# Attention and two feed-forward layers on one core: probability transposes ahead of the scores in odd steps, and another order of the PSUM pools

## The chip, the core and the metric

The kernel runs on one core of a Trainium2 chip. The metric is the device time of one launch in microseconds (us). Three runs of the kernel before gave 614.35, 614.77 and 615.74, median 614.77. TensorE (PE) multiplies and transposes and can write only to PSUM, here eight banks of 128 x 512 fp32; VectorE (DVE) and ScalarE (ACT) read PSUM; GpSimd (POOL) works in SBUF; SyncE (SP) issues DMAs.

## The reference

```python
scores = scale * np.matmul(q, k.transpose(0, 1, 3, 2))   # 2 batches, 8 heads, 768 positions, 64 wide
keep = is_sink | in_window                               # 4 sink keys, window of 128
scores = np.where(keep, scores, -1000000000.0)
a = np.exp(scores - max); a = a / (sum + 1e-09)
x = (a @ v), heads side by side                          # 1536 x 512
h = np.maximum(x @ w_in, 0.0); x = h * h @ w_out         # 512 -> 2048 -> 512
h = x @ w_in2; out = (h * np.tanh(softplus(h))) @ w_out2
```

All inputs and the result are fp32. The feed-forward products run with each factor split into a high and a low fp32r part, three products for one.

## The kernel before, in words

**Attention.** The 1536 rows are 12 tiles of 128 (two batches of six). Each tile has four head pairs, so there are 48 pairs; with a window of 128 and a few sink keys a pair needs scores of 128 queries against 128 keys (first tile of a batch), 256 (second tile) or 208 (all others, in two halves of 64 queries). The loop at L574 is a software pipeline over steps n = -3 to 52, written out by hand; every engine's queue holds its instructions in the order in which the steps issue them. Step n issues, in this order:

- `emit_s` (L398): scores of pair n+4 on PE, two PSUM banks;
- `emit_exp` (L419): exp of pair n+3 on ACT, PSUM to SBUF;
- `emit_max` (L409): mask and row maximum of pair n+4 on DVE, in PSUM, with the value `nm` that the exp needs;
- in even steps `emit_rs` (L430, L431, DVE) and `emit_norm` (L439, POOL): the reciprocal sums and the normalisation of pairs n+2 and n+3;
- `emit_x` (L503 ACT, L504 and L506 POOL) when the tile of pair n-4 is complete: the tile's result `av` is copied to `xf` and split;
- in odd steps `emit_t` (L451): PE transposes the probabilities of pairs n-1 and n, 64 x 64 at a time, into two banks; the first transpose writes the first bank, the second the other, and so on in turn;
- in even steps `prep_rows` (L346; PE transposes q and k of a later tile into two banks, which ACT and DVE copy out, L354) where n = 2 modulo 4 and such a tile is left (n = 2, 6, ..., 38), and then `emit_av` (L488): the products of pairs n-4 and n-3 with v, summed in one bank per tile;
- `evac_t` (L466): the two banks of transposed probabilities are copied to SBUF, the first by ACT, the second by DVE. They are copied in step n itself for n = 1 modulo 4, and in step n+1 for n = 3 modulo 4.

**Feed-forward layers.** `moe` follows with its own order: for each block of 128 hidden units 12 products h (L195, one bank), the activation on ACT and DVE (L204 to L209), and 12 products o (L659, four banks that accumulate over a stage). The h of the first two blocks is computed inside the attention loop, in steps 46 and 48, in banks of the scores' pool (`early[0]`, `early[1]`); ACT squares it in the step after and DVE takes the low part (L209) in the second step after. So `moe` begins with the o products of block 0, then h of block 2, then o of block 1. The weights are loaded by SP, and converted by ACT and DVE (L128 to L171) all the while.

**PSUM.** Pools take banks in the order in which they are opened. Before: `ps_s` (scores and early h) banks 0 to 3, `ps_p` (all transposes) 4 to 6, `ps_a` (av) 7. When the attention's pools are closed, `ps_h` takes 0 to 3 and `ps_o` 4 to 7. Inside a pool, as the program is built, the tiles get the first bank, then the last, then the last but one and so on down to the second, and then the first again: scores 0, 3, 2, 1; transposes 4, 6, 5; the four o tiles 4, 7, 6, 5. A new tile in a bank waits until the last reader of the old one is done, across pools too. 96 score tiles come before the two early h, which therefore get the first and the last bank of `ps_s`. In the ring of three for the transposes each `emit_t` of a step 4t+1 has as its second bank the first bank of step 4t-1; `prep_rows` of step 4t+2 has as its second bank the first of step 4t+1; `emit_t` of step 4t+3 has as its second bank the first of `prep_rows`. All three of these first banks are copied out by ACT.

Of the kernel before, what the change touches and what calls it, by code (L numbers as in the profile page):

```python
# [16 lines left out]
PSUM = bass.MemoryType.PSUM  # L17
# [11 lines left out]
def kernel(  # L29
# [41 lines left out]
    def load_limits():  # L71
        for j, src in enumerate((n_sink, window)):
            nc.scalar.dma_start(out=raw_i[:, j, :], in_=src.bitcast(I32).partition_broadcast(1))
# [137 lines left out]

    att = ExitStack()
    apool = att.enter_context(tc.tile_pool(name="apool", bufs=1))
    ps_s = att.enter_context(tc.tile_pool(name="ps_s", bufs=4, space=PSUM, reuse_waits="tile"))
    ps_p = att.enter_context(tc.tile_pool(name="ps_p", bufs=3, space=PSUM, reuse_waits="tile"))
    ps_a = att.enter_context(tc.tile_pool(name="ps_a", bufs=1, space=PSUM, reuse_waits="tile"))

    tiles = [(b, i) for b in range(B) for i in range(NB)]
    qn, kn, vn = {}, {}, {}
# [1 line left out]
    def load_tile(t, names="qkv", halves=1):  # L221
        if t >= len(tiles):
            return
        b, i = tiles[t]
        hs = H // halves
        for nm in names:
            dst = {"q": qn, "k": kn, "v": vn}[nm]
            dst[b, i] = apool.tile([P, H, D], F32, tag=nm + "n", name=nm + "n", bufs=5 if nm == "v" else 3)
        for h in range(0, H, hs):
            for nm in names:  # L230
                src, dst = {"q": (q, qn), "k": (k, kn), "v": (v, vn)}[nm]
                nc.sync.dma_start(
                    out=dst[b, i][:, h : h + hs, :],
                    in_=src[b, h : h + hs, i * P : (i + 1) * P, :].rearrange("h p d -> p h d"),
                )
# [18 lines left out]
    def positions():  # L254
        make_identity(nc, ident)
        for dst, base, pattern, mult in (
            (rel, 0, [[-1, P]], 1), (col, 0, [[1, P]], 0), (relp, P, [[-1, P]], 1)
        ):
            nc.gpsimd.iota(
                dst, pattern=pattern, base=base, channel_multiplier=mult, allow_small_or_imprecise_dtypes=True  # L260
            )
            if dst is rel:
                nc.gpsimd.affine_select(
                    out=rel, in_=rel, pattern=pattern, base=base, channel_multiplier=mult,
                    compare_op=ALU.is_ge, fill=1.0e9,
                )
# [25 lines left out]
    def load_rest(t):  # L292
        if t >= len(tiles) or tiles[t][1] < 2:
            return
        b, i = tiles[t]
        x = vx[b, i] = apool.tile([KV, 2, H, D], F32, tag="vx", name="vx", bufs=4)
        for dst, r, r0, n in (
            (0, 0, 0, SK), (SK, 0, i * P, HQ), (0, 1, i * P - HQ, HQ), (HQ, 1, 0, SK)
        ):
            nc.sync.dma_start(  # L300
                out=x[dst : dst + n, r], in_=v[b, :, r0 : r0 + n, :].rearrange("h p d -> p h d")
            )
# [65 lines left out]
    def chunks(i):  # L368
        if i == 0:
            return ((None, 0), (None, 0))  # L370
        if i == 1:
            return ((0, P), (0, P))
        return ((0, P), (0, KV))
# [67 lines left out]
    def emit_t(group):  # L441
        banks = [ps_p.tile([P, 2, 2, 2, P // 2], F32, tag="pt", name="pt") for _ in range(2)]
        for s, (b, i, j) in enumerate(group):
            for e in range(2):
                for c in range(2):
                    for r in range(2):
                        o = chunks(i)[r][c]
                        if o is None:
                            continue
                        rows = slice(r * D, (r + 1) * D)  # L450
                        nc.tensor.transpose(  # L451
                            banks[r][:, s, c, e, :], pr[b, i][rows, 2 * j + e, o : o + P], ident[rows, rows]
                        )
        pts = apool.tile([P, 2, 2, 2, P], F32, tag="pts", name="pts", bufs=2)
        for s, p in enumerate(group):
            st["pts", p] = pts[:, s]
        st["evac"] = [(group, banks[r], pts[..., r * D : (r + 1) * D], r) for r in range(2)]
# [72 lines left out]
    with tc.manual_schedule():  # L530
        load_limits()
        nc.scalar.preload_act_table_set("natural_log_exp_and_others")
        load_tile(0, "qk", halves=2)
        load_tile(1, "qk")
        load_tile(2, "kq")
        load_tile(0, "v")
        load_tile(3, "kq")
        positions()
        load_tile(1, "v")
        load_tile(2, "v")  # L540
        load_rest(2)
        warm = apool.tile([P, P], F32, name="warm")
        nc.vector.memset(warm, 0.0)
        nc.vector.memset(one, 1.0)
        nc.gpsimd.memset(two, 2.0)
        for x in prs:
            nc.gpsimd.memset(x[:, :, WIN:], 0.0)
        for x in sums:
            nc.vector.memset(x, 1e-9)
        idle = ps_a.tile([P, P + 2], F32, tag="av", name="idle")  # L550

        def keep_warm(times):
            for _ in range(times):
                nc.tensor.matmul(idle[:, 0:P], lhsT=warm, rhs=warm, start=True, stop=True)  # L554

        keep_warm(WARM[0])
        limits(idle[:, P : P + 2])
        first_mask()
        prep(0, "q", 0)
        keep_warm(WARM[1])  # L560
        prep(0, "k", 0)
        keep_warm(WARM[2])
        emit_s(*pairs[0])
        emit_max(*pairs[0], 0)
        emit_max(*pairs[0], 1)
        prep(0, "q", 1)
        prep(0, "k", 1)
        emit_s(*pairs[1])
        emit_max(*pairs[1], 0)
        emit_max(*pairs[1], 1)  # L570
        second_mask()
        window_masks()
        emit_exp(*pairs[0])
        for n in range(-3, NPR + 5):  # L574
            at = {d: pairs[n + d] for d in range(-4, 5) if 0 <= n + d < NPR}
            last = {d for d in at if at[d][2] == NPAIR - 1}
            t, j = divmod(n, NPAIR)
            if 4 in at and n > -3:
                emit_s(*at[4])
            if 3 in at and n > -3:  # L580
                emit_exp(*at[3])
            if 4 in at and n > -3:
                emit_max(*at[4], 0)
            if 4 in at and n > -3:
                emit_max(*at[4], 1)
            if n % 2 == 0:
                split_x()
                group = [at[d] for d in (2, 3) if d in at]
                if group:
                    emit_rs(group)  # L590
                for p in group:
                    emit_norm(*p)
            if -4 in last:
                emit_x(*at[-4][:2])

            if n % 2:
                if 0 in at:
                    emit_t([at[-1], at[0]])
            else:
                if n >= 0 and j == 2:  # L600
                    prep_rows(t + 2)
                for d in (-4, -3):
                    if d in at:
                        emit_av(*at[d])
            for _ in range((2, 2, 0, 0)[j]):
                evac_t()
            if n in (-3, -2):
                prep(1, "qk"[n + 3])
            if n >= 0 and j == NPAIR - 1:
                load_tile(t + 4, "q", halves=1 + (t + 5 == len(tiles)))  # L610
                load_tile(t + 4, "k", halves=1 + (t + 6 >= len(tiles)))
                load_tile(t + 3, "v")
                load_rest(t + 3)
            if n in SINKS:
                sink_keys(SINKS[n])
            if n < 0:
                keep_warm(WARM[3])
            if n == 1:
                fast_flag()
            for fb in range(W1N):  # L620
                if n == IN_AT[fb]:
                    early[fb] = ps_s.tile([P, TS], F32, tag="s", name="h")
                    in_products(early[fb], wt[0, fb], 0)
                if n == IN_AT[fb] + 1:
                    ready[fb] = new_g(gpool)
                    relu_squared(early[fb], ready[fb][0])
                if n == IN_AT[fb] + 2:
                    low_part(early[fb], *ready[fb])
            for m, steps in PLAN.items():
                for step in steps.get(n, "").split():  # L630
                    getattr(blocks[m], step)()
# [416 lines left out]
```

## Time and profile before

| | |
|---|---|
| median of three runs | 614.77 us |
| the profiled execution: time, span of its instructions | 614.9 us, 613.1 us |
| PE busy | 605.3 us (99%) |
| DVE, ACT, POOL busy | 452.1, 349.8, 70.6 us |
| DMA | 49.47 MB, mean 81 GB/s |
| granted TensorE clock, mean | 0.999 |

The attention stage takes about the first 90 us of the span, the feed-forward layers the rest. The time is the span and what lies around it, 1.8 us here. In rows of a timeline the columns are start, duration, engine, line, operation, output<-inputs, shape and count, and in brackets how long the engine had been idle and what released it. A group of PE instructions can contain waits: eight score products of one form that mostly take 0.58 us and once 0.99 us have waited inside. The chain of waits lists what the end of the program goes back to, in order of time: start, duration, engine, tile, line, count. There a PE row counts from one end to the next, so its length is the pace, and added idle time shows as a longer row.

### The profile page before, as it was taken

What the parts mean: (1) busy time and instruction counts of PE and PEld (TensorE: products, weight loads), DVE (VectorE), ACT (ScalarE), POOL (GpSimd) and SP (SyncE); (2) the same over time, 40 slices, a digit from 0 to 9 for tenths busy, and PEclk for the clock granted to TensorE, in tenths of its full rate; (3) what the DMA queues carried; (4) which work ended last, traced back from release to release, by engine and by line L of the source; (5) the groups of instructions that cost most, each with busy time, mean ns of one, the idle gap of its engine ahead of it and who ended that gap; (6) DMA issues with size and microseconds to landing.
All of it is one profiled execution on the core that took longest, in us unless ns stands there. A gap on an engine that the chain in (4) does not pass through costs nothing.

```text
span 613.1 us, 10262 instructions
## 1 busy us (share of the span) xinstructions
PE 605.3 (99%) x3854; PEld 491.6 (80%) x3854; DVE 452.1 (74%) x951; ACT 349.8 (57%) x723; POOL 70.6 (12%) x103
## 2 busy tenths in 40 slices
PE   9999999999999999999999999999999999999996
PEld 6676778888888888888888888888888888888885
DVE  5888889999621111188899699999888778888784
ACT  5989876877643333277777555555454444544442
POOL 5889950000000000000000000000000000000000
PEclk9999999999999999999999999999999999999999
DMA  9989736666400000036666300000010000100001
GB/s 188 188 181 185 196 108 202 207 204 187 158 1 0 2 0 1 0 111 198 204 196 188 101 0 2 0 1 1 1 69 1 0 1 0 53 17 2 0 1 72
DMA packets 71707, 49.47 MB, mean 81 GB/s; under 512 B 49508, under 2 KB 66148, under 8 KB 71652
## 3 DMA queue, kind: packets, MB, share of 16 engines
q1 hardware_dynamic: 71360, 48.38, 28.8%
q8 instruction: 31, 0.51, 0.4%
q10 hardware_dynamic: 292, 0.39, 0.2%
q14 instruction: 24, 0.20, 0.1%
HBM read 45.61 MB, written 3.15 MB: 80 GB/s over the span
## 4 chain that ended last, share of the span: by engine, by line
PE 96%; ACT 2%; DMA 1%; DVE 1%; issue 0%; DVEq 0%; ACTq 0%; SPq 0%
PE o L659 43%; PE h L195 42%; PE s L398 4%; PE av L488 3%; PE pt L451 2%; PE tr L346 1%; PE idle L554 1%; DMA raw<-in_moe_w_out_dram 1%; ACT pr L419 0%; PE tr L328 0%; ACT pts L466 0%; DVE cv_r L142 0%; ACT h L205 0%; ACT xf L503 0%; ACT h L204 0%
## 5 line engine op out<-in xcount | busy, mean ns | idle before, releaser
L195 PE MATMUL h<-xh,wil 128*128 128x512 f32 x384 | 102.9, 390 | 0.0
L195 PE MATMUL h<-xl,wih 128*128 128x512 f32 x384 | 102.7, 389 | 0.0
L195 PE MATMUL h<-xh,wih 128*128 128x512 f32 x384 | 102.6, 389 | 0.0
L209 DVE TENSOR_TENSOR gl<-h,gh 128x512 fp32r<-128x512 f32 x48 | 33.2, 691 | 89.0 <-ACT gh L206 88.9
L195 PEld LDWEIGHTS h<-xl,wih 128*128 128x128 f32 x384 | 72.1, 188 | 15.0
L195 PEld LDWEIGHTS h<-xh,wih 128*128 128x128 f32 x384 | 72.1, 188 | 15.0
L195 PEld LDWEIGHTS h<-xh,wil 128*128 128x128 f32 x384 | 71.9, 188 | 15.0
L659 PE MATMUL o<-gh,wol 128*128 128x512 f32 x192 | 74.9, 390 | 0.6 <-ACT xf L503 0.5
L727 ACT ACTIVATE e<-t,small 128x512 f32<-128x512 f32 x48 | 34.8, 725 | 70.4 <-DVE t L723 70.4
L659 PE MATMUL o<-gl,woh 128*128 128x512 f32 x192 | 74.7, 389 | 0.0
L659 PE MATMUL o<-gh,woh 128*128 128x512 f32 x192 | 74.7, 389 | 0.0
L204 ACT ACTIVATE h<-h 128x512 f32<-128x512 f32 x48 | 28.0, 582 | 76.1 <-PE h L195 76.1
L659 PE MATMUL o<-wol,gh 128*128 128x512 f32 x176 | 68.5, 389 | 0.0
L659 PE MATMUL o<-woh,gl 128*128 128x512 f32 x176 | 68.5, 389 | 0.0
L659 PE MATMUL o<-woh,gh 128*128 128x512 f32 x176 | 68.5, 389 | 0.0
L743 ACT CAST gh<-t 128x512 fp32r<-128x512 f32 x44 | 27.4, 623 | 46.3 <-PE o L659 42.9
L148 DVE SCALAR_TENSOR_TENSOR cv_a<-cv_a,cv_r 128x512 int32<-128x512 int32 x64 | 44.7, 698 | 6.2
L209 DVE TENSOR_TENSOR gl<-t,gh 128x512 fp32r<-128x512 f32 x44 | 30.4, 690 | 19.8 <-ACT gh L743 19.8
L128 ACT ACTIVATE cv_a<-raw 128x512 f32<-128x512 f32 x63 | 42.4, 673 | 1.5 <-DMA raw<-in_moe_w_out_dram 0.9
L659 PEld LDWEIGHTS o<-gh,wol 128*128 128x128 f32 x192 | 36.0, 187 | 8.5 <-ACT xf L503 1.0
L419 ACT ACTIVATE pr<-s,nm 128x208 f32<-128x208 f32 (+2 forms) x96 | 40.8, 438 | 2.4 <-DVE nm L409 2.2
L439 POOL TENSOR_TENSOR pr<-pr,rs 128x416 f32<-128x416 f32 (+2 forms) x48 | 41.0, 875 | 10.0 <-DVE rs L431 5.3
(107 smaller groups left out, 1000.5 us busy)
## 6 DMA issues: line engine op xcount, KB each, us to landing
raw<-in_moe_w_in_dram SPq DMA_DIRECT2D x32, 512.0 KB, 4.0
raw<-in_moe_w_out_dram SPq DMA_DIRECT2D x32, 512.0 KB, 4.3
vn<-in_v_dram SPq DMA_DIRECT2D x12, 256.0 KB, 5.7
qn<-in_q_dram SPq DMA_DIRECT2D x10, 256.0 KB, 4.8
kn<-in_k_dram SPq DMA_DIRECT2D x9, 256.0 KB, 5.1
vx<-in_v_dram SPq DMA_DIRECT2D x16, 128.0 KB, 4.1
out_dram<-ob SPq DMA_DIRECT2D x8, 256.0 KB, 2.4
kn<-in_k_dram SPq DMA_DIRECT2D x6, 128.0 KB, 3.3
```

The costliest lines, as they stand in the source:

```text
L128: nc.scalar.activation(out=self.a, in_=high_words, func=AF.Copy, scale=2.0**-112)
L148: nc.vector.scalar_tensor_tensor(out=ai, in0=ai, scalar=3, in1=self.r, op0=ALU.logical_shift_left, op1=ALU.bitwise_or)
L195: nc.tensor.matmul(ph, lhsT=w[a][:, d, :], rhs=x[:, d, :], start=(m == 0 and d == 0), stop=(m == 2 and d == NDC - 1),)
L204: nc.scalar.activation(out=ph, in_=ph, func=AF.Relu)
L209: nc.vector.tensor_tensor(out=gl, in0=x, in1=f32(gh), op=ALU.subtract)
L398: nc.tensor.matmul(banks[e][qs, 0:w], lhsT=kt[r, j, q1], rhs=kt[r, j, k0 : k0 + w], start=True, stop=True, skip_group_check=True,)
L419: nc.scalar.activation(out=pr[b, i][:, 2 * j + e, 0:w], in_=banks[e][:, 0:w], func=AF.Exp, bias=nm[:, e : e + 1], scale=-1.0, accum_out=sm ...
L439: nc.gpsimd.tensor_tensor(out=x, in0=x, in1=rs.to_broadcast([P, 2, w]), op=ALU.mult)
L488: nc.tensor.matmul(av[b, i][e * D : (e + 1) * D, j, qs], lhsT=x[0:kv, 2 * j + e, :], rhs=pts[0:kv, c, e, qs], start=(j == 0 and m == 0), s ...
L659: nc.tensor.matmul(acc[sp][t], lhsT=a, rhs=x, start=(fb == 0 and m == 0), stop=(fb == NFB - 1 and m == 2),)
L727: nc.scalar.activation(out=e, in_=t, func=AF.Ln, bias=two)
L743: nc.scalar.copy(g_tiles(n)[0], et[n][1])
```

## The change

Two edits. The pool `ps_a` is opened ahead of `ps_s`: av is then in bank 0, the scores and early h in 1 to 4 (taken in the order 1, 4, 3, 2), the transposes in 5 to 7. `ps_h` and `ps_o` are opened as before and keep 0 to 3 and 4 to 7. And in odd steps `emit_t` is issued at the head of the step, ahead of `emit_s`; everything else keeps its place in the step, `evac_t` too.

```diff
     apool = att.enter_context(tc.tile_pool(name="apool", bufs=1))
+    ps_a = att.enter_context(tc.tile_pool(name="ps_a", bufs=1, space=PSUM, reuse_waits="tile"))
     ps_s = att.enter_context(tc.tile_pool(name="ps_s", bufs=4, space=PSUM, reuse_waits="tile"))
     ps_p = att.enter_context(tc.tile_pool(name="ps_p", bufs=3, space=PSUM, reuse_waits="tile"))
-    ps_a = att.enter_context(tc.tile_pool(name="ps_a", bufs=1, space=PSUM, reuse_waits="tile"))
...
             t, j = divmod(n, NPAIR)
+            if n % 2 and 0 in at:
+                emit_t([at[-1], at[0]])
             if 4 in at and n > -3:
                 emit_s(*at[4])
...
-            if n % 2:
-                if 0 in at:
-                    emit_t([at[-1], at[0]])
-            else:
+            if n % 2 == 0:
                 if n >= 0 and j == 2:
                     prep_rows(t + 2)
```

## Rows read from the trace of the kernel before

**Rows 1.** The page: busy time by engine, and the chain by engine.

```profile
PE 605.3 (99%) x3854; PEld 491.6 (80%) x3854; DVE 452.1 (74%) x951; ACT 349.8 (57%) x723; POOL 70.6 (12%) x103
...
PE 96%; ACT 2%; DMA 1%; DVE 1%; issue 0%; DVEq 0%; ACTq 0%; SPq 0%
```

**Rows 2.** Stages: length, busy us of PE, PEld, DVE, ACT, POOL, granted clock, DMA.

```profile
28.91:47.92 19.01, 18.84 (x438) 14.22 (x436) 16.02 (x72) 16.73 (x65) 16.29 (x21) 1.00 0.94 191
80.55:93.43 12.88, 12.15 (x121) 9.31 (x118) 11.65 (x21) 9.90 (x18) 4.01 (x5) 1.00 0.50 164
```

**Rows 3.** Chain of waits in the attention stage: start, us, what.

```profile
26.29 1.02 PE av L488 x16
...
33.74 0.51 PE s L398 x8
34.25 0.64 PE pt L451 x16
...
35.41 1.08 PE av L488 x32
...
38.16 0.20 PE tr L346
...
38.37 0.71 PE tr L346 x15
...
44.52 0.71 PE tr L346 x15
...
50.59 0.64 PE tr L346 x16
...
53.80 0.59 PE av L488 x8
54.39 0.92 PE s L398 x8
...
56.59 0.81 PE tr L346 x16
```

**Rows 4.** Timeline of DVE, the maximum of a step 4t+3.

```profile
34.30 0.38 DVE L409 CUSTOM_DVE_ANT_0 s<-s,mask_w 128x208 f32<-128x208 f32 x1 [0.51 <-PE s L398]
```

**Rows 5.** Timeline of ACT, steps 3, 16 and 17.

```profile
14.83 0.58 ACT L354 COPY kt<-tr 128x512 f32<-128x512 f32 x1 [0.20 <-PE tr L346]
...
34.77 0.43 ACT L419 ACTIVATE pr<-s,nm 128x208 f32<-128x208 f32 x1 [0.23 <-DVE nm L409]
...
35.61 0.58 ACT L466 COPY pts<-pt 128x512 f32<-128x512 f32 x1
...
37.73 0.58 ACT L466 COPY pts<-pt 128x512 f32<-128x512 f32 x1 [0.69 <-PE pt L451]
```

**Rows 6.** Timeline of PE, steps 22, 31 and 45.

```profile
44.11 0.87 PE L346 MATMUL tr<-ident,kn 64*128 64x64 f32 x8
...
58.42 0.73 PE L451 MATMUL pt<-ident,pr 64*128 64x64 f32 x16
...
78.60 0.94 PE L451 MATMUL pt<-ident,pr 64*128 64x64 f32 x16
```

**Rows 7.** Timeline of POOL, normalisation of pairs 30 to 33.

```profile
56.60 3.72 POOL L439 TENSOR_TENSOR pr<-pr,rs 128x512 f32<-128x512 f32 x4
```

**Rows 8.** Timeline where the feed-forward layers begin, PE and PE's weight loads.

```profile
89.77 0.50 PE L659 MATMUL o<-gh,wol 128*128 128x512 f32 x1
...
91.25 0.19 PEld L659 LDWEIGHTS o<-gh,wol 128*128 128x128 f32 x1 [0.95 <-ACT xf L503]
91.25 0.50 PE L659 MATMUL o<-gh,wol 128*128 128x512 f32 x1 [0.52 <-ACT xf L503]
...
93.43 1.09 PE L195 MATMUL h<-xh,wil 128*128 128x512 f32 x4
```

**Rows 9.** The same stretch on ACT and DVE.

```profile
90.61 0.59 ACT L503 COPY xf<-av 128x512 f32<-128x512 f32 x1
90.75 0.69 DVE L209 TENSOR_TENSOR gl<-h,gh 128x512 fp32r<-128x512 f32 x1
```

## The prediction

> **What bounds the kernel now.** I read the page first. PE is busy for 605.3 of 613.1 us and holds 96% of the chain that ended last [rows 1]: an edit moves the time only if it opens or closes a gap on PE. The second view was busy time by stages. The granted clock is 1.00, the 2.4 GHz level, both inside attention and where the feed-forward layers begin [rows 2], so I charge nothing for the clock. In attention ACT, POOL and DVE have 84 to 88% of the stage as busy time and PE 99%: PE sets the pace, but the others have little room. The third view, the chain of waits, gives PE's pace piece by piece [rows 3]. Free of waits, the scores of a 208-wide pair cost 0.51, the transposes of two pairs 0.64, av 1.08 (1.02 or 0.59 where a tile has fewer keys), and prep_rows 0.64. A typical tile of four steps should cost 4 x 0.51 + 2 x 0.64 + 2 x 1.08 + 0.64 = 6.1 us.
>
> The losses are visible as longer rows. In step 18 the first of the 16 transposes of prep_rows ends the free run after 0.20, and the other 15 take 0.71: 0.92 in place of 0.64 [rows 3]. ACT's row shows why: it waited 0.69 for the transposed probabilities of step 17, began to copy their first bank at 37.73 and ended at 38.31 [rows 5], and that bank is prep_rows' second. The same loss of 0.28 stands at steps 10, 14, 34 and 38 (step 6 I take with the start). Step 22 loses 0.4 (begun at 44.11, the last 15 run from 44.52 [rows 3, 6]), step 30 loses 0.17 (0.81 [rows 3]); the scores of step 29 wait 0.41 for an exp (0.92 [rows 3]) and those of step 30 about 0.1.
>
> **The change, part by part.**
>
> *What the move can free.* With emit_t ahead, ACT gets the transposes of steps 4t+1 one score block, 0.51, earlier, and the 0.69 for which it now waits [rows 5] lets it use that. prep_rows' wait goes, and the scores, now 0.64 later, find their exp done. Sum of the losses above: 5 x 0.28 + 0.4 + 0.17 + 0.41 + 0.1 = 2.5 us. No instruction is added or removed, no DMA moves, and no queue but PE's changes its order.
>
> *What is late next.* emit_t of step 4t+1 needs as its second bank the first bank of step 4t-1. ACT copies that in step 4t, behind the exp of pair 4t+3, whose scores are the last thing that step 4t-1 now puts on PE. Call T the end of those scores. The chain behind T is in the rows of step 15: scores end at 33.74 + 0.51 = 34.25 [rows 3]; DVE starts at 34.30, having waited for them [rows 4]; the exp starts at 34.77, having waited for DVE; the copy runs from 35.61 to 36.19 [rows 5]. That is T + 1.94, and PE resumes some 0.04 later: T + 1.98. The same chain recurs to within 0.02 in steps 19, 35 and 39. Before, PE had scores behind it three times over: transposes, scores, av, scores, 2.74 in all, so no wait showed. After, only the scores and av of step 4t lie between: 0.51 + 1.08, and 0.04 for the first transpose, 1.63. The second transpose waits 1.98 - 1.63 = 0.35, with the even step's work queued behind it on PE.
>
> By step: 0.41 in step 9 and 33 (av 1.02), 0.35 in 13, 17, 37 and 41, 0.48 in 21 (scores of 128 keys precede it, by their width some 0.38), 0.05 in 25, and 0.65 in 29, where av is 0.59: 0.51 + 0.59 + 0.04 = 1.14 against a chain that I estimate at 1.79, since the copy there is of half a bank. Together 3.4 us.
>
> A wait on PE also costs a restart. In step 18 the 15 transposes after the wait take 0.71, where 15/16 of 0.64 is 0.60 [rows 3]: 0.11. Eight of these waits are long enough to count: 0.9. Its bounds are 0, if the restart hides, and 0.28, the whole loss of prep_rows; I take the measured 0.11.
>
> The Trainium skill says in TensorE: Matmul & The Clock Gate, section "Architectural detail: the array is 16× 32×32, not 1× 128×128", that PE's queue is a partial reorder window which can pull weight loads ahead of matmuls in flight; by that the weights would be in place when a wait ends, and the restart would be free. The trace does not agree for a wait on a semaphore: where PE waits for xf, the weight load and its matmul both start at 91.25 [rows 8].
>
> *emit_t of step 4t+3* needs the bank that prep_rows filled and ACT copies out behind an exp that ends the same chain, so about T' + 1.98, T' being the end of the scores of step 4t+1. PE is there at T' + 0.51 + 0.64 + 1.08 + 0.04 = 2.27: covered, with 0.3 to spare. Not so where av is 0.59 (1.78): 0.2 + 0.11 in step 31.
>
> *The start.* In step 3 ACT copies prep_rows' bank from 14.83 to 15.41 [rows 5], and the transposes would begin at about 14.8: they wait 0.6. The score block behind them is then 0.6 late, which the old wait of step 4's scores for an exp absorbs; but step 5's transposes then wait 0.7 for the bank of step 3 (same chain, av 0.59), step 6 gets its 0.28 back, and step 7 waits 0.3. Following the pieces to the end of step 7 I get 22.7 against 22.2: +0.5, with 0 and +1 as its ends.
>
> *Step 45.* No scores are left in step 44, so only av (1.08) covers the chain: 1.98 - 1.12 = 0.86, and 0.11. Its transposes take 0.94 already, 0.24 over the 0.71 usual for this row's form [rows 6]: +0.7. Low end 0.3, if DVE and ACT, which have less to do there, shorten the chain.
>
> *The bank of av.* Before, the o products stop after the first three, because the second o tile lies in av's bank and waits for xf, which ends at 91.20; PE goes on at 91.25 [rows 8, 9]. After, av's bank goes to h of block 2, which PE reaches later than 91.20, so this wait goes. But the first o tile now takes bank 4, and that was the scores' second slot: it holds early[1] until DVE has taken its low part, 90.75 to 91.44 [rows 9]. PE is ready at 89.77. All twelve products then start at about 91.48 and take 0.34 + 11 x 0.23 = 2.85, to 94.33; now h starts at 93.43 [rows 8]: +0.9. Its ends: 0.6, if DVE gets to that low part sooner, and 1.2, if ACT and DVE run later against PE.
>
> *Sum:* -2.5 + 3.4 + 0.9 + 0.3 + 0.5 + 0.7 + 0.9 = +4.2 us. From 93.43 on PE has no gap, so nothing is given back. The profiled execution took 614.9, 0.1 over the median: 619.1 on its scale, 619.0 on that of the median.
>
> **The rivals.**
>
> *Only the bank costs.* The new waits are as long as the old ones: DVE and ACT, relieved in the even steps, shorten the chain by some 0.2 at each of nine places, and restarts hide. Attention is level, the o products pay 0.9: 615.8. For it: in most chains ACT and DVE have idle time just before [rows 4, 5]. Against: that idle time is the wait for the scores themselves, so it cannot shorten what comes after them.
>
> *Faster.* The copy of step 4t-1's bank is done before PE needs it. Price: the 2.5 us freed, with 0.9 paid for the bank, 613.3. It decides at 1.63 us behind the scores; the four chains read all stand at 1.94. What speaks for it is only the 0.69 of ACT.
>
> *POOL becomes the bound.* The scores of odd steps come 0.64 later and the transposes 0.51 earlier, so the normalisation between has 1.15 less. Where POOL keeps up that is spare, but the four of pairs 30 to 33 run without a break from 56.60 to 60.32 [rows 7], and step 31's transposes began at 58.42 [rows 6], when the second of their pairs had just become ready. If steps 31, 33, 35 and 45 each lose 0.5 more: 621.0. Against: each bank wait ahead of them gives POOL time.
>
> *Restarts are free*: ten times 0.11 less, 617.9; against it stands the weight load at 91.25 [rows 8]. This is what the skill's rule above would give.
>
> **How the numbers follow.** The forecast 0.55 (own range 617.1, with the restarts, the start and step 31's restart at nothing and step 45 at 0.3, to 620.1, with the start at +1 and the losses of steps 22 and 30 left), free restarts 0.08, only the bank 0.17, faster 0.09, POOL 0.11. The range runs from 615.5 to 620.8: below it lie the faster case and a little of the level one, above it most of the POOL case's upper half. A measurement of this kernel tells about 0.2%, 1.2 us, from no change: faster 0.09; same 0.16, which is the level case but for a little; slower 0.75.
>
> **What would show it.** In the changed kernel's trace prep_rows should be 16 transposes in 0.64 without a break, and PE should wait for ACT's copies (L466) inside the transposes of steps 4t+1, by 0.35 to 0.65. The first o product should be released by DVE's low part (L209), none by xf, and start some 1.7 us after the last av; h of block 2 should start near 97.6. The prediction is wrong if the transposes run without such waits (then the faster case), if what releases them is mostly POOL, or if the o products start right behind av.

## The result, and the profile after

The changed kernel took 620.13 us (median of six runs, 618.63 to 621.37) against 615.2 for the kernel before in the same session (614.35 to 615.89, six runs): 1.0079 times as long, 95% interval 1.0057 to 1.0101. It is slower by 4.9 us where +4.2 was forecast; 619.0 lies inside the runs, but not in their middle, since they form two groups: 618.63, 618.86, 619.03 and 621.23, 621.35, 621.37. The profiled execution is one of the upper group (621.37, span 619.6). Why there are two is the part that the prediction lacks.

First the page after, the two rows that answer to [rows 1]:

```profile
PE 604.6 (98%) x3854; PEld 495.9 (80%) x3854; DVE 452.0 (73%) x951; ACT 350.3 (57%) x723; POOL 70.7 (11%) x103
...
PE 91%; ACT 3%; DVE 3%; issue 1%; POOL 1%; DVEq 0%; ACTq 0%; POOLq 0%
```

Each engine does what it did, to within 1%; 6.5 us of span are added, and the chain now leaves PE for 9% of its length, before for 4%: there PE waits for what other engines still do. The same nine tiles of attention, from the first prep_rows of step 2 to that of step 38, as windows (length, busy us of PE, PEld, DVE, ACT, POOL, granted clock, DMA), first before, then after:

```profile
14.09:68.66 54.57, 54.37 (x1084) 38.20 (x1081) 47.17 (x214) 48.84 (x180) 47.71 (x61) 1.00 0.90 182
```

```profile
14.99:72.33 57.34, 52.16 (x1083) 40.24 (x1081) 46.31 (x210) 49.41 (x180) 47.29 (x60) 1.00 0.82 172
```

PE's idle time in the stretch goes from 0.20 to 5.18 us, and the stretch grows by 2.8. PE's busy time falls by 2.2, in part because waits that used to stand inside rows counted as busy (the 0.92 of prep_rows, [rows 3]) are gone, in part because score blocks that now stand back to back take less (below). What PE waited for, over the whole span (us, times, longest):

```profile
PE pt L451 <- ACT pts L466: 4.4, 9, 0.8
PE o L658 <- DVE gl L209: 1.9, 1, 1.9
PE idle L554 <- DVE warm L543: 1.1, 1, 1.1
PE pt L451 <- ACT kt L354: 0.9, 2, 0.6
PE av L488 <- ACT xf L503: 0.7, 1, 0.7
PE s L398 <- ACT pr L419: 0.3, 1, 0.3
```

The second row comes with the pools; the first, fourth and fifth come with the order, since the kernel with the order alone has the same three (below); the other two stand before the change as well. A typical tile in the chain of waits, to be read against [rows 3]:

```profile
36.43 0.58 PE s L398 x8
37.01 0.36 DVE s L409
37.37 0.07 DVE nm L409
37.47 0.94 ACT pr L419 x4
38.41 0.48 ACT pts L466
...
38.94 0.71 PE pt L451 x15
39.65 0.86 PE s L398 x16
40.51 0.64 PE tr L346 x16
41.15 1.08 PE av L488 x32
```

prep_rows is whole again (16 in 0.64), and in its place the second transpose of step 17 ends a chain scores, maximum, exp, copy. The scores end at 37.01 and the transposes resume at 38.94: T + 1.93. The row `0.86 PE s x16` is new: without transposes between them the scores of an odd step and those of the next even step stand back to back and take 0.86 together, not 2 x 0.51.

The junction with the feed-forward layers, PE's timeline (start, us, ..., idle before, releaser), to be read against [rows 8]:

```profile
93.34 0.29 PE L488 MATMUL av<-pts,vn 128*64 128x64 f32 x4
95.50 0.70 PE L658 MATMUL o<-gh,wol 128*128 128x512 f32 x1 [1.87 <-DVE gl L209]
96.00 0.63 PE L658 MATMUL o<-gl,woh 128*128 128x512 f32 x1
...
98.99 0.43 PE L658 MATMUL o<-gh,woh 128*128 128x512 f32 x1
99.25 0.39 PE L658 MATMUL o<-gh,wol 128*128 128x512 f32 x1
...
99.95 0.39 PE L195 MATMUL h<-xh,wil 128*128 128x512 f32 x1
```

and three windows around it:

```profile
93.56:95.50 1.94, 0.07 (x4) 0.00 (x0) 1.85 (x4) 1.91 (x5) 0.56 (x1) 1.00 0.32 106
95.50:99.25 3.75, 3.75 (x9) 2.94 (x10) 3.52 (x7) 2.27 (x5) 0.06 (x1) 0.54 0.58 163
99.25:102.00 2.75, 2.75 (x13) 2.25 (x12) 2.58 (x6) 1.13 (x2) 0.00 (x0) 1.00 0.61 193
```

PE waits 1.87 us for the low part of `early[1]`; then the granted clock is 0.54 of full, mostly the 1.2 GHz level, and the products follow one another at 0.43 in place of 0.23: eight times 0.2, 1.6 us. Then it is at 2.4 GHz again. The next row of the chain, h of block 2, starts 6.5 us later than before (99.95, 93.43 [rows 8]), and from there to the end of the span both take 519.7 (619.6 less 99.95, 613.1 less 93.43).

### The profile page after: what moved, and what is told of

It is laid out like the page before. It is cut to its first block, busy times and chain, and to the rows that moved or that the text cites. A ratio compares the mean times of both kernels' runs of the same rounds, so it can differ in the third digit from the quotient of the medians.

```text
span 619.6 us, 10254 instructions
## 1 busy us (share of the span) xinstructions
PE 604.6 (98%) x3854; PEld 495.9 (80%) x3854; DVE 452.0 (73%) x951; ACT 350.3 (57%) x723; POOL 70.7 (11%) x103
## 4 chain that ended last, share of the span: by engine, by line
PE 91%; ACT 3%; DVE 3%; issue 1%; POOL 1%; DVEq 0%; ACTq 0%; POOLq 0%
PE o L658 42%; PE h L195 41%; PE s L398 2%; ACT pr L419 2%; PE pt L451 2%; PE idle L554 1%; PE av L488 1%; DVE s L409 1%; ACT pts L466 1%; PE tr L346 1%; POOL pr L439 1%; PE tr L328 0%; DVE cv_r L142 0%; DVE cv_a L148 0%; DVE pts L466 0%
## 5 line engine op out<-in xcount | busy, mean ns | idle before, releaser
L658 PEld LDWEIGHTS o<-gh,woh 128*128 128x128 f32 x192 | 36.5, 190 | 7.7
L439 POOL TENSOR_TENSOR pr<-pr,rs 128x416 f32<-128x416 f32 (+2 forms) x48 | 41.0, 876 | 14.2 <-ACT pr L419 7.4
```

Source lines behind the costliest of these rows:

```text
L439: nc.gpsimd.tensor_tensor(out=x, in0=x, in1=rs.to_broadcast([P, 2, w]), op=ALU.mult)
L658: nc.tensor.matmul(acc[sp][t], lhsT=a, rhs=x, start=(fb == 0 and m == 0), stop=(fb == NFB - 1 and m == 2),)
```

## The experiments

In the table "path" is worked out from each profile: from the start of the first scores on PE to the start of the first h of block 2. It leaves out the very beginning, which differs between profiles by up to 1.3 us for the same code (last section); behind it all spans are within 0.5 us of 519.6. The kernel before had medians of 614.84 to 615.18 in the sessions of the experiments.

| kernel | median us (range, runs) | to before, 95% | path us |
|---|---|---|---|
| before | 614.84 to 615.18 | | 86.98 |
| after | 620.13 (618.63 to 621.37, 6) | 1.0057 to 1.0101 | 92.61 |
| order only | 618.02 (617.85 to 618.82, 5) | 1.0036 to 1.0062 | 89.78 |
| pools only | 617.10 (615.32 to 618.24, 12) | 1.0015 to 1.0041 | 89.29 |
| ahead in 4t+1 only | 614.60 (613.53 to 616.16, 11) | 0.9985 to 1.0005 | 86.09 |
| ahead in 4t+3 only | 618.94 (618.28 to 619.44, 5) | 1.0050 to 1.0076 | 90.30 |
| after, copy first | 617.27 (614.70 to 618.71, 12) | 1.0010 to 1.0039 | 88.62 |
| pools, tiny matmul | 615.10 (614.26 to 615.98, 11) | 0.9991 to 1.0008 | 86.55 |
| 4t+1, pools, tiny matmul | 614.79 (613.58 to 616.16, 11) | 0.9985 to 1.0002 | 86.03 |
| after, PE kept busy (8) | 619.47 (618.59 to 620.10, 5) | 1.0055 to 1.0081 | 91.06 |
| after, copy first, tiny matmul | 614.63 (613.45 to 615.30, 11) | 0.9980 to 0.9997 | 85.84 |
| 4t+1, copy first, tiny matmul | 613.67 (612.70 to 615.06, 10) | 0.9965 to 0.9988 | 85.07 |
| after, again | 619.77 (618.79 to 621.50, 6) | 1.0061 to 1.0095 | 91.84 |
| after, PE kept busy (4) | 619.42 (618.32 to 620.07, 5) | 1.0059 to 1.0085 | 91.02 |

**Order only**: the pools as before, the transposes ahead.

```diff
-    ps_a = att.enter_context(...)      # opened ahead of ps_s
     ps_s = ...
     ps_p = ...
+    ps_a = att.enter_context(...)
```

> The transposes ahead in all odd steps, the pools as before. Theory (each emit_t of a step 4t+1 waits for ACT's copy behind the exp of the scores that now come last in step 4t-1): the waits for L466 stand as in the changed kernel, nine of them, some 4.4 us, prep_rows is free of waits, and the attention stage costs about 3.0 us: 618.0. The first o products run and then wait for xf, by about 0.7 as before, which is too short for the clock to fall, so all runs lie within about 1 us of one another. Rival (the bank of av makes most of the loss): within 1 us of before. Rival (POOL is the bound): as slow as the theory says, but the waits inside the transposes are released by L439.

618.02, one group, +3.2 us: the order without the bank is what the prediction's terms without the bank make (+3.3). The nine waits for ACT's copies stay at 4.4 us, the wait for gl is gone.

**Pools only**: the pools as after, the transposes where they were.

> The pools in the new order, emit_t where it was. Theory: attention as before, the first o product waits for DVE's low part (L209) and h of block 2 comes 0.9 us later: 615.9 where the clock stays up; in a share of the runs it falls behind this wait, which costs 8 x 0.2 = 1.6 us more: 617.5. Rival (the loss of the junction comes only with the late attention): no wait there, 615.0. Rival (the clock's fall has its cause elsewhere): runs in one group.

Two groups again: five runs at 615.3 to 616.0, six at 617.2 to 618.2, and one between. Its PE waits for gl as the changed kernel does:

```profile
PE o L659 <- DVE gl L209: 1.9, 1, 1.9
```

The median of its lower group, 615.66, is 0.8 above the kernel before, near the 0.9 that was charged for the bank; its upper group is 3 above. So the second group comes with the bank, not with the order.

**One odd step at a time.** The pools as before; first the transposes ahead in the steps 4t+1 alone, then in 4t+3 alone.

```diff
+            if n % 4 == 1 and 0 in at:     # or n % 4 == 3
+                emit_t([at[-1], at[0]])
             if 4 in at and n > -3:
                 emit_s(*at[4])
...
-                if 0 in at:
+                if 0 in at and n % 4 == 3:     # or n % 4 == 1
                     emit_t([at[-1], at[0]])
```

> Pools as before; emit_t ahead of the scores in steps 4t+1 alone. Theory: the scores of step 4t-1 end 0.64 earlier than in the changed kernel, so 0.64 + 0.51 + 1.08 + 0.04 = 2.27 lie behind them against a chain of 1.98: no wait for L466 in the 1.08 tiles, and prep_rows' waits go: 2.0 to 2.5 us faster than before, 613. Rival (transposes ahead of scores cost by themselves, by POOL or by late scores): half of the loss of the whole reorder, 616.5.

> Pools as before; emit_t ahead of the scores in steps 4t+3 alone. Theory: 0.51 + 1.08 + 0.51 + 0.04 = 2.14 lie between the scores of step 4t-1 and the second transpose of step 4t+1, against 1.98: no wait in the 1.08 tiles, but prep_rows keeps its losses; steps 3, 5, 29, 31 and 45 lose some 1.7 together: 616.7. Rival (each of the two moves costs by itself): half of the loss, 616.5, with waits for L466 in most tiles.

Both missed their figures, and together they tell where the nine waits come from. They appear in the steps 4t+1. But moved alone these steps cost nothing: the path is 0.9 shorter than before, a typical tile takes 5.94 to 5.98 (before 6.36 to 6.43) unless one of the remaining waits stands in it (6.49 with that of step 13), and of the nine waits three are left, 1.3 us:

```profile
PE pt L451 <- ACT pts L466: 1.3, 3, 0.8
```

ACT's timeline tells why, first with 4t+1 alone, then the changed kernel, both around step 16:

```profile
35.91 0.43 ACT L419 ACTIVATE pr<-s,nm 128x208 f32<-128x208 f32 x1
...
36.75 0.58 ACT L466 COPY pts<-pt 128x512 f32<-128x512 f32 x1
```

```profile
37.47 0.43 ACT L419 ACTIVATE pr<-s,nm 128x208 f32<-128x208 f32 x1 [0.50 <-DVE nm L409]
...
38.30 0.58 ACT L466 COPY pts<-pt 128x512 f32<-128x512 f32 x1
```

With the scores of step 4t+3 ahead of its transposes, as before, ACT finds its maxima ready and copies 0.68 us before the transposes of step 17 start (37.43 there). With the scores behind them ACT stands idle for 0.50 and its copy starts when these transposes do (38.30). So the move in 4t+3 makes the copy late; the wait shows only where the move in 4t+1 makes PE need that copy early. With 4t+3 alone there is one wait for L466, 0.6 in step 45.

The move in 4t+3 alone cost 4.1 (path +3.3), more than both moves together. Typical tiles take what they took before (6.35, 6.41); the loss stands at the start, at the end, and where a tile has fewer keys and less work of PE covers the chain. It is not taken apart further here. The largest single one is in step 26, in PE's timeline:

```profile
51.32 1.11 PE L398 MATMUL s<-kt 64*64 64x256 f32 x8 [0.81 <-ACT pr L419]
```

That the time of 4t+1 alone (614.60, 0.2 below before) shows less than its path's 0.9 is not settled: its profile begins 0.9 later than that of before, and whether its other runs do is not in the traces.

**Copy first.** The changed kernel; in steps 4t ACT copies the bank ahead of its exponentials.

```diff
                 emit_s(*at[4])
+            if j == 0:
+                evac_t()
             if 3 in at and n > -3:
                 emit_exp(*at[3])
...
-            for _ in range((2, 2, 0, 0)[j]):
+            for _ in range((1, 2, 0, 0)[j]):
```

> The changed kernel with one more move: in the steps 4t ScalarE copies the first transposed probabilities before its exponentials, not behind them; the other copies stay. My theory: the transposes of the steps 4t+1 waited for ScalarE because that copy stood behind four exponentials; the waits 'PE pt <- ACT pts' (4.4 us over nine) go, and the run ends 3 to 4 us before the changed kernel: 615.0 to 615.9 where the product with wo keeps its clock, 617.5 to 618.4 where it does not. Rival: ScalarE has no slack in these steps, the exponentials come .48 later and the scores of the next step wait for their bank instead ('PE s <- ACT pr' rises from .3 to 3 us or more): 618.3 to 621, as the changed kernel.

The waits for ACT's copies of pts are gone and the rival's waits for exp stay at 0.3. Four runs lie at 614.7 to 615.1 and eight at 617.2 to 618.7, about as expected (the lower group a little below), 3.8 to 4.0 below the changed kernel's groups: the chain through that one copy is the price of the new order.

**A tiny matmul in step 47.** The kernel before with the new pool order, and one more tile of the score pool, so that `early[1]` falls into another bank than the first o tile. Then the same with the transposes ahead in 4t+1.

```diff
+            if n == IN_AT[0] + 1:
+                gap = ps_s.tile([P, TS], F32, tag="s", name="gap")
+                nc.tensor.matmul(gap[:, 0:2], lhsT=warm, rhs=warm[:, 0:2], start=True, stop=True)
```

> The kernel before with the new order of the PSUM pools, and one tiny matmul (two columns) into an additional tile of the score pool in step 47, so that the first product with wo meets a bank that is free early. If the wait of 1.9 us for VectorE's gl is what the new pool order costs, both it and the low clock behind it go: no wait for gl over .3, granted clock 1.00 in the 4 us behind the first o, all runs in one group at 613.7 to 614.6 (before: 614.84), that is 2.5 to 3 below the pools alone (617.1). Rival: the new order costs elsewhere (another bank shared): 615.3 to 617.5 still.

> Transposes ahead in the steps 4t+1 alone, the new pool order, and the tiny matmul in step 47. The order in 4t+1 alone gained about 1 us by step 43 and gave it back at the end of the attention, where av waits for ScalarE and for the weights' conversion on VectorE. If that chain still sets the end and only the bank is new: 613.6 to 614.4, below both kernels. If the two gains hide each other: 614.6, as with either alone.

The wait for gl and the upper group are both gone, 2.0 us below the pools alone (617.10). But the expected gain did not come: 615.10 is the kernel before. The wait for xf that [rows 8] shows, and that the new order of the pools does remove, gave nothing back that can be measured; the path is 0.4 shorter, and behind the o products the first h now waits for the weights' low part:

```profile
PE h L195 <- DVE wil L171: 0.3, 1, 0.3
```

With 4t+1 ahead as well 614.79 is not told from before either; the path (86.03) is as short as with 4t+1 alone, so the two gains do not add.

**TensorE kept busy.** The changed kernel with eight matmuls whose result is unused behind the last av, later with four.

```diff
+            if n == NPR + 3:
+                fill = ps_s.tile([P, TS], F32, tag="s", name="fill")
+                for _ in range(8):             # or 4
+                    nc.tensor.matmul(fill[:, 0:P], lhsT=warm, rhs=warm, start=True, stop=True)
```

> The changed kernel with eight matmuls of 128 columns (result unused) into an additional tile of the score pool behind the last av, so that TensorE works in a part of the 1.87 us for which the first product with wo waits for gl. If the low clock after that wait comes from TensorE's standing idle, no run shows a stretch at .54 there and all runs lie in the changed kernel's lower group, 618.4 to 619.9 (the upper part where the start is .9 slower). If the clock falls for another reason, half the runs stay at 621.2 to 621.5. The additional tile may also shift which score bank o meets: then the wait for gl goes and 616.5 to 618 comes out, which says the same of the clock only by its rows.

> The changed kernel with four of the unused matmuls of 128 columns behind the last av in place of eight, so that TensorE stands idle for about .9 us of the 1.87 before the first product with wo. If a shorter idle stretch is enough to keep the clock: all runs at 618.4 to 620.1 and no low clock in the profile, as with eight. Rival: any gap can do it: two groups still, 618.6 to 619 and 620.5 to 621.4.

With eight (1.95 us) PE has no idle time ahead of the first o. With four, 0.82 is left. Neither has a run in the upper group, ten runs in all, where the changed kernel has five of twelve at 621.0 or more, and the pools alone half. The window behind the first o, with eight and with four, to be read against the 0.54 above:

```profile
95.30:98.18 2.88, 2.88 (x14) 2.36 (x14) 2.66 (x5) 1.54 (x3) 0.05 (x1) 1.00 0.57 178
```

```profile
94.43:97.28 2.85, 2.85 (x13) 2.36 (x13) 2.66 (x5) 1.51 (x3) 0.02 (x1) 1.00 0.57 175
```

Twelve products in 2.85 to 2.88, the 2.85 of the prediction, at full clock. Useless work makes the kernel no slower (619.47 and 619.42 against 620.13 and 619.77) and takes its upper group away: here the low clock follows from standing idle.

**The changed kernel again**, unchanged.

> The changed kernel once more, for a second profile and more times. Its times lie in two groups 2.5 us apart (618.6 to 619.0, 621.2 to 621.4); the one profile, of the upper group, shows 1.6 of it as eight products at half clock behind the wait for gl, and starts .9 later than the kernel before. Mine: the lower group has neither the low clock nor the late start: if its profile is of that group, the granted clock behind the first o is 1.00 and the first scores stand at 6.3 to 6.5. Rival: the start has nothing to do with it: scores at 7.3 in the lower group too, and .9 of the gap is elsewhere. If the profile is of the upper group again, scores at 7.3 and a clock of about .5 behind the wait. In either case both groups appear in its times.

Both groups are there (618.79, 618.81, 618.97; 621.09, 621.50) and a run at 620.58, which is the one profiled. It waits as long and keeps its clock:

```profile
96.35 0.50 PE L658 MATMUL o<-gh,wol 128*128 128x512 f32 x1 [1.78 <-DVE gl L209]
96.69 0.40 PE L658 MATMUL o<-gl,woh 128*128 128x512 f32 x1
```

```profile
96.35:99.20 2.85, 2.85 (x12) 2.36 (x13) 2.52 (x5) 1.66 (x3) 0.15 (x1) 1.00 0.55 174
```

So an idle stretch of this length lets the clock fall in some runs and not in others. Every run also has a mean granted clock of its span, and it divides the three kernels with this wait (changed, pools only, copy first) as their times do: the 19 runs of the upper groups have 0.996 or 0.997, the other 17 runs 0.999 or 1.000. A stretch of 3.75 us at 0.54 takes 0.003 off the mean of such a span. A low clock at the very end of a span enters this mean as well, so it supports the reading without counting the falls by itself.

The half of the theory on the clock is thus borne out. The half on the start is not settled: the run has the late start (7.36) without the low clock, and no profile of the lower group was had. Beside the late start it takes 0.9 longer than the first profile from step 38 to step 48, which is why it lies above the lower group all the same. The nearest is that with four matmuls, 618.32, with full clock and an early start (6.26); low clock (1.6) and late start (0.9) would add up to the gap of 2.5.

**Both kernels beaten.** The remedies together: copy first and the tiny matmul on the changed kernel, and the same with the transposes ahead in the steps 4t+1 alone.

> The changed kernel with ScalarE's copy ahead of the exponentials in the steps 4t, and the tiny matmul in step 47 that gives the first product with wo another bank. From the first scores to the first h of block 2 the copy-first kernel took 88.6 us (before: 87.0) with 1.9 of waiting for gl and eight products at half pace (1.6) in it; without these 85.1 to 86.0 are left. Mine: no wait for gl, no low clock, all runs in one group, and .5 to 1.2 under the kernel before: 614.0 to 614.7 where that is 615.2. Rival: the end of the attention is held by ScalarE's xf and the weights' conversion whatever the transposes do (as the tiny matmul alone, 615.1): no gain.

> Transposes ahead in the steps 4t+1 alone, new pool order, tiny matmul in step 47, and ScalarE's copy ahead of the exponentials in the steps 4t. Ahead in 4t+1 alone still waited 1.3 us for that copy in three steps. Mine: two of these waits go (the third, step 29, is .8 for the window's length) and 614.2 to 614.7 comes out against 614.8 without the copy's move. Rival: the later exponentials cost as much in the scores of 4t+1 ('PE s <- ACT pr' over 1 us): 614.8 to 615.8.

The first is 0.1% under the kernel before, as expected. The second is at 613.67 the fastest: 0.9977 of before, 0.9965 to 0.9988, and below what was expected. All its waits for ACT's pts are gone, that of step 29 too, which was expected to stay; what PE still waits for behind the start is:

```profile
...
PE av L488 <- ACT xf L503: 0.5, 1, 0.5
PE s L398 <- ACT pr L419: 0.3, 1, 0.3
PE o L666 <- DVE wol L171: 0.3, 1, 0.3
PE pt L451 <- POOL pr L439: 0.2, 1, 0.2
PE tr L346 <- DVE nm L409: 0.2, 1, 0.2
```

and a typical tile in its chain is PE alone, 5.98 from av to av:

```profile
32.63 1.08 PE av L488 x32
33.71 0.51 PE s L398 x8
34.23 0.64 PE pt L451 x16
34.87 0.51 PE s L398 x8
35.38 1.08 PE av L488 x32
36.46 0.64 PE pt L451 x16
37.11 0.86 PE s L398 x16
37.97 0.64 PE tr L346 x16
```

## Why the prediction was right, and where it was not

The sign and the size came from the right mechanism. Taken by its steps:

- **prep_rows freed: right.** 0.64 without a break in every typical tile.
- **The waits in steps 4t+1: right in place, nearly right in sum, in part by luck.** Forecast 0.41 in steps 9 and 33, 0.35 in 13, 17, 37, 41, 0.48 in 21, 0.65 in 29, with 0.11 of restart each; the profile has 0.50 and 0.42, four times 0.36, 0.49, 0.79, and 15 transposes in 0.71 behind each (the ninth wait, step 5's, is part of the start). But two things in that step were off and cancel. The scores of step 4t cost PE 0.3 behind those of 4t-1, not 0.51, since they stand back to back; so PE comes earlier and stands longer. In step 17 the transposes take 1.28 until the next scores start, where 0.64 is free:

```profile
38.30 0.27 PE L451 MATMUL pt<-ident,pr 64*128 64x64 f32 x1
...
39.58 0.94 PE L398 MATMUL s<-kt 64*64 64x208 f32 x16
```

  That is 0.64 lost, of which the profile counts 0.36 as idle, and not 0.35 + 0.11. Against it stands a gain that the sum lacked: 0.16 at each pair of score blocks that stand back to back, two pairs in a tile. So a typical tile loses less than the 0.18 forecast for it (0.46 less the 0.28 of prep_rows): from prep_rows to prep_rows the three from steps 10, 14 and 34 take 6.51, 6.45 and 6.43, before 6.36, 6.43 and 6.36. Most of the 2.8 us by which the nine tiles grow stands in the two tiles from step 2 to step 10 (1.3) and in the one from step 30 to step 34 (0.9).
- **The cause within the pair of odd steps: right chain, but not followed to its use.** The prediction says that the scores of 4t-1 come last; it did not draw from it that moving 4t+1 alone would be free. That 4t+3 alone costs as much as both, by other waits, it did not see either.
- **The start: right in its waits, a little low in sum.** 0.61, 0.74, 0.28 in steps 3, 5 and 7 (forecast 0.6, 0.7, 0.3). From the first prep_rows to the av of step 8 it is 0.67 longer (9.19, before 8.52), where 0.5 was forecast up to the end of step 7.
- **Step 31: too low.** Charged 0.3 for ACT; the row of its transposes is 1.39 long, before 0.73 [rows 6], and POOL released the last of them:

```profile
60.49 1.39 PE L451 MATMUL pt<-ident,pr 64*128 64x64 f32 x16
```

  The chain leaves POOL's L439 at 61.37. That is the POOL rival's mechanism, 0.66 at this one step; steps 33 and 35 did not follow, so POOL did not become the bound.
- **Step 45: right in sum by luck, wrong in place.** 0.7 was charged to its transposes; in the first profile they did not wait (0.94 as before [rows 6]), and the av of step 44 ahead of them lost 0.69 to ACT's xf. In the second it was 0.39 on that av, 0.25 on the transposes and 0.50 on the av of step 48.
- **The bank: right where the clock holds.** Charged 0.9, measured 0.8 by the pools alone.
- **"I charge nothing for the clock": the step that failed.** The forecast had PE idle for 1.7 us there and took the clock of [rows 2] for granted after it. In about half of the runs it was not. The mis-sized term is the bank's: 0.9 in some runs, 3 in others. By the lower group (618.63 to 619.03) the sum hit within 0.4 us; the median of 620.13 is the mean of 619.03 and 621.23, one run of each group. The Trainium skill says in TensorE: Matmul & The Clock Gate, section "HAM oscillation — how this bites in real kernels", that waits of TensorE can put its clock back to the lower level, so that the next work starts slow; the kernel measured there waits longer than this one. The traces here agree that it happens, by 0.54 behind a wait of 1.87, and show that at this length it need not, by 1.00 behind one of 1.78.

Of the rivals, free restarts fell with the 15 transposes that take 0.71 behind each wait; as in [rows 8], the weight load of the first o also starts with its matmul, at 95.50. "Only the bank" and "faster" fell with the order alone (+3.2). Two slips in the working change nothing: 0.34 + 11 x 0.23 is 2.87 and not 2.85, and the rivals' 615.8 and 613.3 start from the profiled execution, the forecast of 619.0 from the median.

## What to carry to other kernels

When instructions of one engine change places, follow what the later ones feed, through every engine, to where it comes back: here scores that were 0.64 late returned two steps on as a bank that was not yet copied, and moving one copy on another engine took the waits away with the change kept; the fastest version undoes the move in steps 4t+3 as well. Count a new wait of TensorE as long as the one here (1.8 to 1.9 us) twice, once as idle time and once as the work behind it at the lower clock in some of the runs; here a few unused matmuls, which left 0.82 of the wait, or a free bank avoided the second. Look for blocks of one kind that a move lets stand back to back: two score blocks cost 0.86 and not 1.02, and that is a part of the 0.4 us by which a typical tile of the fastest version is shorter (5.98, before 6.36 to 6.43).

## What the runs showed that I had not expected

The clock's fall is a matter of the run, not of the program alone: the same kernel, the same wait of 1.8 to 1.9 us, 0.54 behind it in one profile and 1.00 in the other.

The beginning varies as well, with the same code ahead of it. Six matmul instructions that keep TensorE busy at 4.9 us take 0.83 us in the profile of before and 1.49 in that of the changed kernel:

```profile
4.93 0.83 PE L554 MATMUL idle<-warm 128*128 128x128 f32 x6
```

```profile
4.97 1.49 PE L554 MATMUL idle<-warm 128*128 128x128 f32 x6
```

The first scores start at 6.45 and 7.34, and between 6.26 and 7.52 over all profiles. That is as large as the gains at stake, so a single profile compares kernels only from a common point on.

The granted clock of a window reads 1.00 there in both, but only because a stretch for which a trace has no record of the clock counts as 1.00. The first record, at 1.00, starts at 4.88 us in the trace of before and at 6.88 in that of the changed kernel. Until then these instructions follow one another at 0.21 us and from then on at 0.11, nearly as 1.2 GHz stands to 2.4. Over the 14 traces that record starts between 4.08 and 7.32, and the later it starts, the later stand the first scores, to within 0.01 us. So a late start is a longer stretch at the slow pace; why the clock rises earlier in one run than in another stays open.
